# A planner with two DMA queues: beacon attention and a gated feed-forward part on one core

## The chip, the core and the metric

The kernel runs on one core of a Trainium2 chip, as one launch. The metric is the device time of that launch in microseconds. Five engines have an instruction queue each: TensorE (PE in the profile), VectorE (DVE), ScalarE (ACT), GpSimd (POOL) and SyncE (SP); transfers are started from SP's queue (the hardware queue q1 of the profile) and from POOL's (the software queue q0).

## The reference

```python
B, H, S, Nb, D = (8, 8, 576, 16, 64)
k_all = np.concatenate([beacon_k, k], axis=2)
v_all = np.concatenate([beacon_v, v], axis=2)
scores = scale * np.matmul(q, k_all.transpose(0, 1, 3, 2))
causal[:, Nb:] = np.triu(np.ones((S, S), dtype=bool), k=1)
scores = np.where(causal, -1000000000.0, scores)
a = np.exp(scores - scores.max(-1, keepdims=True))
a /= a.sum(-1, keepdims=True) + 1e-09
attn_out = np.matmul(a, v_all)
x = attn_out.transpose(0, 2, 1, 3).reshape(B * S, H * D)      # 4608 x 512
gate = np.maximum(x @ w_gate, 0.0)                             # 512 x 1536
return (gate * (x @ w_val)) @ w_out                            # 1536 x 512
```

All inputs and the output are float32.

## The kernel before

Attention is worked batch by batch (eight batches), two pairs of heads at a time (`quad`, g = 0 and 1). Queries, keys and values are loaded through eight staging tiles `st`, rounded to bf16 on GpSimd (in batch 0 also on VectorE), keys and queries are turned on TensorE (`turned`, line 538) and copied out of PSUM into `kT` and `qT`. Scores (line 809) are masked and their row minimum of the negated scores is taken on VectorE (757), exponentials come from ScalarE (764), reciprocals from VectorE (770), and the normalisation by GpSimd (775). The probabilities are transposed, on TensorE in batch 0 (885) and else by a DMA transpose on SP's queue (895), and multiplied by the values (905, 928). The results go to `xT`, from which the feed-forward part reads spans of 240 to 512 tokens: gate (966) and value products (971), their product on VectorE (982), the output product (997), an eviction and a store (1011).

The order of all this on every engine is not written by hand. Each piece is a `Task` with its engines, a modelled cost, what it depends on, the buffers that it holds and a priority; `Plan.order` simulates the program and emits each task when its turn comes. So what the planner believes about durations decides what stands ahead of what in each engine's queue, and each queue is worked in order on the chip. Where the plan has TensorE idle in the first part, it puts in filler matmuls on a spare bank (`fill`, line 1049). Value products of later batches may lie up to `LAZY` = 20 us behind feed-forward matmuls.

Transfers in the planner before: one number `wire` says when all that was issued will have moved. A load adds its `move` to it and lands `LAND` = 1.8 us later; weights, issued by GpSimd, add theirs to the same number. A new transfer waits until the wire is at most `BACKLOG` = 6 us ahead. Weights become due at `W0 + W_STEP * i`.

`HELD` names three loads of batch 1 that wait for the issue of a given weight, and `BEHIND` one load of batch 2 that waits for normalised probabilities of batch 1: the staging tile is first written by a one-element memset on GpSimd (548), and the load depends on that.

The batch's loads go in the order of a string: `K` and `Q` are the rest of the keys and queries, a digit a pair of heads (keys first, then queries), `v` one block of 128 value rows (the fifth has 80):

```python
for what in ORDER0 if b == 0 else "KQ0011v2233vvvv":
```

Of the kernel before, what the change touches and what calls it, by code (L numbers as in the profile page):

```python
# [12 lines left out]
ALU = mybir.AluOpType  # L13
# [22 lines left out]
TURN = (7,)  # L36
QUADS = 5
TLAZY = 8.0
TURN_FIRST = 100
TURN_LOAD = 1.5  # L40
# [15 lines left out]
W_ROWS = 4  # L56
W0 = 14.0
W_STEP = 1.4
W_ISSUE = 0.85
W_MOVE = 0.72  # L60
V_MOVE = 1.25
LAND = 1.8
N_ST = 8
# [10 lines left out]
VCAST = 9  # L74
STORES = 0

# [81 lines left out]
class Task:  # L158
    def __init__(self, engines, cost, run, deps, holds, prio, lag, part=0, lazy=0.0, move=0.0):
# [21 lines left out]


class Plan:

# [5 lines left out]

    def add(self, engines, cost, run, deps=(), holds=(), prio=0.0, lag=None, part=0, lazy=0.0, after=0.0, move=0.0):
        t = Task(engines if isinstance(engines, tuple) else (engines,), cost, run, deps, holds, prio, lag, part, lazy, move)
        t.ready = after
        for d in t.deps:
            d.users.append(t)
        self.tasks.append(t)
        return t

    def order(self):
        free = {}  # L200
        queue = {}
        for t in self.tasks:
            for e in t.engines:
# [6 lines left out]
        wire = 0.0  # L210
        part = 0
        free["DMA"] = 0.8
        done = []

        def begin(t, e):
            at = t.ready
            if e == "DMA" or t.move:
                at = max(at, wire - self.backlog)
            for h in t.holds:
                if h.tile is None:  # L220
                    if h.prev is not None:
                        continue
                    if h.next is not None:
                        first = h.slots.first_pairs(sum(x.next is not None for x in t.holds))
# [8 lines left out]
            return max(at, free[e]), at  # L233

        while True:
            best = None
            for e in queue:
                for t in queue[e]:
                    times = begin(t, e)
                    if times is None:  # L240
                        continue
                    at, could = times
                    late = 0
                    if e == "PE":
                        late = -1 if part and t.part == part else NEXT if part and t.part else 1 if part != t.part and at < t.ready + t.lazy else 0
                    key = (at, late, t.prio)
                    if best is None or key < best[0]:
                        best = (key, t, e)
            if best is None:
                break  # L250
# [19 lines left out]
            if e == "DMA":  # L270
                issue, move = cost
                if issue > 1.2:
                    wire = max(wire, at + 0.3) + move
                    free[e] = max(at + issue, wire - 0.2)
                else:
                    free[e] = at + issue
                    wire = max(wire, at + issue) + move
                end = max(wire, free[e]) + LAND
            else:
                if isinstance(cost, dict):  # L280
                    cost = cost[e]
                if e == "PE":
                    cost += SWITCH * (t.part != part)
                    part = t.part
                free[e] = end = at + cost
                if t.move:
                    wire = max(wire, end) + t.move
                    end = wire + LAND
            for h in t.holds:
                h.users -= 1  # L290
                if h.users == 0:
                    h.slots.give(end + (0.1 if e == "DMA" else LAGS[e] if t.lag is None else t.lag), h.tile)
            done.append(t)
            for u, then in [(u, end) for u in t.users] + [(u, free[e]) for u in t.soon]:
                u.ready = max(u.ready, then + (LAGS[e] if t.lag is None else t.lag))
                u.left -= 1
                if u.left == 0:
                    for x in u.engines:
                        queue[x].append(u)
        assert all(t.start is not None for t in self.tasks)  # L300
# [5 lines left out]
def kernel(  # L306
# [102 lines left out]
    def c_pool(n):  # L409
        return 0.245 + 0.00083 * n  # L410

    def c_pe(n):
        return 0.003 + n / 2400.0
# [74 lines left out]
    def weight(kind, ko, kos, n0, w, prio, work):  # L488
        d, s = {"g": (wg_r, wg_s), "v": (wv_r, wv_s), "o": (wo_r, wo_s)}[kind]
        x = add("POOL", W_ISSUE, lambda t: nc.gpsimd.dma_start(  # L490
            d[:, ko:ko + kos, n0:n0 + w], s[:, ko:ko + kos, n0:n0 + w]), (), (), work, 0.1, move=W_MOVE * kos * w / 512,
            after=W0 + W_STEP * len(weight_in) / KM)
# [13 lines left out]
    def new_batch(b, prio, work):  # L506
# [54 lines left out]
        def load_pair(kind, p, prio):  # L561
# [20 lines left out]
            if b in TURN:  # L582
                t.rows[kind, p] = [add("DMA", (1.22, 0.177 * 4), lambda _: nc.sync.dma_start_transpose(
                    dst.tile[:, p, c0:c0 + MAIN].rearrange("p (j n) -> p j n", j=4), h16.tile), (ca, zeros), (h16, dst), prio[0] - TURN_FIRST)]
                return
# [41 lines left out]
        def load_half(kind, g, half, prio):  # L627
# [24 lines left out]
        def load_rest(kind, prio):  # L652
# [36 lines left out]
        def load_v(c, prio):  # L689
            rows = min(P, SK - P * c)  # L690
            if b >= VCAST:
# [7 lines left out]

                t.rows["v", c] = add("POOL", W_ISSUE * (2 if c == 0 else 1), take, (batches[-1].rows["v", NC - 1],), (t.v,), prio[1], 0.1, move=V_MOVE * rows / P)  # L700
                return
# [31 lines left out]
    def softmax(t, parts, ph, prio, k):  # L733
# [38 lines left out]
        for i, (n, a) in enumerate(whole):  # L772
            def norm(x, i=i, n=n, a=a):
                one = ph.tile.rearrange("p a n -> p (a n)")[:, a:a + n]
                nc.gpsimd.tensor_scalar(one, one, at(8 + i), 1.0, ALU.mult, ALU.mult)  # L775

            outs.append(add("POOL", c_pool(n), norm, (r,), (ph,), prio + 0.001 * i + 0.0005 * k))
        return outs
# [89 lines left out]
    def finish(t, p, vals, ph, pt_s, blocks, on_pe, outs, prio):  # L868
# [89 lines left out]
    def ffn(m0, mt, deps, prio):  # L958
# [26 lines left out]
        for t0 in range(0, mt, P):  # L985
# [19 lines left out]
            for c in range(halves):  # L1005
# [3 lines left out]
                def store(_, c=c, osb=osb[c], rows=rows, t0=t0, w=w):  # L1009
                    q_ = nc.scalar if c or STORES else nc.sync  # L1010
# [72 lines left out]
```

## Time and profile before

| | |
|---|---|
| runs | 398.83, 404.41, 398.99 us; median 398.99 |
| profiled execution | span 403.9 us from first to last instruction; its own time is not listed beside the runs |
| busy | PE 390.9, DVE 282.5, ACT 266.7, POOL 233.8 us |
| mean TensorE clock granted | 0.989 |
| filler matmuls (line 1049) | 89 |
| SP queue q1 / POOL queue q0 | 63.46 MB / 4.72 MB |

The table of stretches gives for each stretch the length, then busy time and count of instructions for PE, PE's weight loads, DVE, ACT and POOL, then the granted clock of TensorE (1.00 is full speed), the mean busy share of the 16 DMA engines and GB/s. With a filter for one line and PE it gives PE alone. In the chain that ended last, each row is a start, a length and what the program's end hung on at that time. In a timeline, the bracket gives the idle time of the engine before the instruction and what ended it. Rows of transfers give count, size of one in KB and the median time from issue to landing.

### The profile page before, as it was taken

What the parts mean: (1) busy time and instruction counts of PE and PEld (TensorE: products, weight loads), DVE (VectorE), ACT (ScalarE), POOL (GpSimd) and SP (SyncE); (2) the same over time, 40 slices, a digit from 0 to 9 for tenths busy, and PEclk for the clock granted to TensorE, in tenths of its full rate; (3) what the DMA queues carried; (4) which work ended last, traced back from release to release, by engine and by line L of the source; (5) the groups of instructions that cost most, each with busy time, mean ns of one, the idle gap of its engine ahead of it and who ended that gap; (6) DMA issues with size and microseconds to landing.
All of it is one profiled execution on the core that took longest, in us unless ns stands there. A gap on an engine that the chain in (4) does not pass through costs nothing.

```text
span 403.9 us, 10330 instructions
## 1 busy us (share of the span) xinstructions
PE 390.9 (97%) x3471; PEld 203.8 (50%) x3471; DVE 282.5 (70%) x1011; ACT 266.7 (66%) x833; POOL 233.8 (58%) x453
## 2 busy tenths in 40 slices
PE   7969999999999989999999999999999999999996
PEld 4636865565454545554454444545444445444543
DVE  3859788897997778878777778678857843442432
ACT  2949879978866776959786787878765841330320
POOL 6877959969793885668687585855670730000000
PEclk9969999999999999999999999999999999999999
DMA  7999894999999899979998999799959655001102
GB/s 181 227 201 244 146 226 145 219 179 233 204 255 202 215 175 259 163 170 276 230 183 225 262 187 159 162 214 158 197 145 193 122 100 152 16 2 52 52 2 91
DMA packets 184101, 68.90 MB, mean 171 GB/s; under 512 B 158384, under 2 KB 179504, under 8 KB 184048
## 3 DMA queue, kind: packets, MB, share of 16 engines
q1 hardware_dynamic: 179216, 63.46, 74.5%
q0 software_dynamic: 4752, 4.72, 7.4%
q8 instruction: 27, 0.44, 0.5%
q14 instruction: 26, 0.21, 0.2%
q10 hardware_dynamic: 80, 0.07, 0.1%
HBM read 38.54 MB, written 9.44 MB: 119 GB/s over the span
## 4 chain that ended last, share of the span: by engine, by line
PE 87%; DMA 5%; ACT 4%; DVE 2%; issue 1%; POOL 0%; ACTq 0%; DVEq 0%
PE f L997 23%; PE f L971 22%; PE f L966 22%; PE f L809 7%; PE f L905 6%; ACT pb L764 3%; PE f L538 3%; DMA st<-in_v_dram 2%; DMA pTa<-pa 2%; PE f L1049 1%; PE f L885 1%; PE f L928 1%; DVE f L757 1%; DMA st<-in_k_dram 1%; PE f L859 1%
## 5 line engine op out<-in xcount | busy, mean ns | idle before, releaser
L775 POOL TENSOR_SCALAR pb<-pb,small 128x320 bf16<-128x320 bf16 (+8 forms) x272 | 141.8, 539 | 69.9 <-DVE small L770 67.3
L764 ACT ACTIVATE pb<-f,small 128x320 bf16<-128x320 f32 (+8 forms) x272 | 144.4, 552 | 22.5 <-DVE small L757 15.1
L757 DVE CUSTOM_DVE_ANT_0 f<-f,mask 128x576 f32<-128x576 f32 (+8 forms) x288 | 134.3, 512 | 13.8 <-PE f L809 6.5
L971 PE MATMUL f<-xT,wv_r 128*128 128x512 bf16 (+3 forms) x480 | 107.4, 358 | 0.0
L966 PE MATMUL f<-xT,wg_r 128*128 128x512 bf16 (+3 forms) x480 | 106.2, 358 | 0.0
L997 PE MATMUL f<-wo_r,hT 128*128 128x512 bf16 (+2 forms) x456 | 102.3, 374 | 0.0
L982 DVE TENSOR_TENSOR hT<-g,f 128x512 bf16<-128x512 f32 (+3 forms) x120 | 75.2, 631 | 36.9 <-PE f L971 33.8
L977 ACT ACTIVATE g<-f 128x512 f32<-128x512 f32 (+3 forms) x120 | 67.7, 567 | 48.3 <-PE f L966 44.3
L966 PEld LDWEIGHTS <-wg_r 128*128 128x128 bf16 x480 | 45.6, 98 | 44.9 <-issue 1.0
L997 PEld LDWEIGHTS <-hT 128*128 128x128 bf16 (+2 forms) x456 | 41.9, 100 | 46.7 <-issue 2.4
L971 PEld LDWEIGHTS <-wv_r 128*128 128x128 bf16 x480 | 43.3, 98 | 42.7 <-issue 3.4
L764 ACT ACTIVATION_READ_ACCUMULATOR pb<-f,small 128x1 f32 x272 | 60.4, 222 | 0.0
L527 POOL TENSOR_SCALAR h<-st 128x512 bf16<-128x512 f32 (+1 forms) x93 | 49.0, 542 | 10.5 <-DMA st<-in_k_dram 3.2
L757 DVE DVE_READ_ACCUMULATOR2_ANT small<- 128x1 f32 x296 | 41.2, 139 | 0.1
L809 PE MATMUL f<-kT,qT 64*64 64x64 bf16 (+7 forms) x640 | 35.9, 296 | 3.4 <-DVE xT L478 3.4
L478 DVE COPY osb<-f 128x512 f32<-128x512 f32 (+1 forms) x29 | 19.7, 681 | 26.9 <-PE f L997 26.8
L476 ACT CAST xT<-f 128x240 bf16<-128x240 f32 (+2 forms) x43 | 15.7, 375 | 25.3 <-PE f L905 24.9
L770 DVE RECIPROCAL small<-small 128x2 f32<-128x2 f32 (+3 forms) x136 | 20.4, 160 | 14.1 <-ACT pb L764 10.4
L809 PEld LDWEIGHTS <-qT 64*64 64x64 bf16 x640 | 14.5, 107 | 27.0 <-issue 22.3
L905 PE MATMUL f<-pTb,v 128*64 128x320 bf16 (+3 forms) x488 | 27.3, 254 | 0.3
L480 POOL TENSOR_SCALAR v<-st 128x512 bf16<-128x512 f32 (+1 forms) x38 | 23.1, 616 | 6.4 <-DMA st<-in_v_dram 6.4
L905 PEld LDWEIGHTS <-v 128*64 128x64 bf16 (+1 forms) x512 | 21.3, 110 | 9.1 <-issue 5.4
(62 smaller groups left out, 231.0 us busy)
## 6 DMA issues: line engine op xcount, KB each, us to landing
out_dram<-osb SPq DMA_DIRECT2D x34, 256.0 KB, 2.5
st<-in_k_dram SPq DMA_DIRECT2D x28, 256.0 KB, 4.6
st<-in_q_dram SPq DMA_DIRECT2D x28, 256.0 KB, 4.4
st<-in_v_dram SPq DMA_DIRECT2D x24, 256.0 KB, 5.3
st<-in_k_dram SPq DMA_DIRECT2D x16, 128.0 KB, 4.1
st<-in_q_dram SPq DMA_DIRECT2D x16, 128.0 KB, 3.2
st<-in_v_dram SPq DMA_DIRECT2D x8, 224.0 KB, 5.3
wg_r<-in_moe_w_gate_dram POOLq DMA_DIRECT2D x3, 512.0 KB, 7.1
```

The costliest lines, as they stand in the source:

```text
L480: nc.gpsimd.tensor_scalar(dst, src, 1.0, 1.0, ALU.mult, ALU.mult)
L527: (nc.gpsimd if x.engine == "POOL" else nc.vector).tensor_scalar(to, src, by, 1.0, ALU.mult, ALU.mult)
L757: nc.vector.tensor_tensor_reduce(out=view(i, n - m), in0=view(i, n - m), in1=msk, scale=1.0, scalar=at(7) if m < n else 3.0e38, op0=ALU.ad ...
L764: nc.scalar.activation(ph.tile.rearrange("p a n -> p (a n)")[:, a:a + n], view(i), AF.Exp, bias=at(i), scale=-1.0, accum_out=at(4 + i))
L775: nc.gpsimd.tensor_scalar(one, one, at(8 + i), 1.0, ALU.mult, ALU.mult)
L809: nc.tensor.matmul(banks[k][b_].tile[64 * i:64 * i + 64, off:off + n], t.q.tile[r, 2 * g + i, 64 * j:64 * j + 64], t.kT.tile[r, 2 * g + i, ...
L905: nc.tensor.matmul(ps.tile[64 * hh:64 * hh + 64, d0:d0 + w], t.v.tile[:rows, c, D * h:D * h + D], rhs(64 * hh), start=(c == 0), stop=(c == ...
L966: nc.tensor.matmul(psg.tile[:, :mt], wg_r[:, ki, nf * P:(nf + 1) * P], xT[:, ki, m0:m0 + mt], start=(ki == 0), stop=(ki == KM - 1))
L971: nc.tensor.matmul(psv.tile[:, :mt], wv_r[:, ki, nf * P:(nf + 1) * P], xT[:, ki, m0:m0 + mt], start=(ki == 0), stop=(ki == KM - 1))
L977: r = add("ACT", c_act(mt), lambda _, psg=psg, g=g: nc.scalar.activation(g.tile[:, :mt], psg.tile[:, :mt], AF.Relu), (a,), (psg, g), -1000 ...
L982: hid.append(add("DVE", c_dve(mt), lambda _, psv=psv, g=g, nf=nf: nc.vector.tensor_mul(hT[nf].tile[:, :mt], g.tile[:, :mt], psv.tile[:, :m ...
L997: nc.tensor.matmul(ps[c].tile[64 * c:64 * c + rows, :w], hT[nf].tile[:, t0:t0 + rows], wo_r[:, nf, w * c:w * c + w], start=(nf == 0), stop ...
```

## The change

The planner gets a class `Wire` with two queues, HW (SP) and SW (GpSimd). Every transfer becomes one or more jobs, each with a number of packets per DMA engine and a kind of packet. A queue works its jobs in order; alone at `ALONE` us per packet, and while both queues have work at the packets per us of `TOGETHER`, first for HW, then for SW. A transfer lands `LAND` after its last packet, and its users are woken by that event. At most eight jobs of the hardware queue are under way. The three holds in `HELD` go; `BEHIND` stays. Weights are due at 13, 16, ... 37 us. All engines start at 0.8 us of the plan. A task that may run on several engines is not given to one where another would finish it sooner. The normalisation takes its engine from `NORM`, which names GpSimd alone, as before. The option `STORES` goes; it was 0.

```diff
-HELD = {(1, 0): ("v", 0, 0), (1, 2): ("g", 0, 1024), (1, 4): ("v", 0, 1024)}
+HELD = {}
-W0 = 14.0
-W_STEP = 1.4
+W0 = 13.0
+W_STEP = 3.0
-W_MOVE = 0.72
-V_MOVE = 1.25
-LAND = 1.8
+LAND = 1.0
+HEAD = {"HW": 0.9, "SW": 1.2}
+ALONE = {256: 0.0182, 512: 0.03, 1024: 0.045, 2048: 0.075, "T": 0.01875, "W": 0.096}
+TOGETHER = {256: (12.0, 9.0), 512: (10.0, 8.7), 1024: (8.0, 8.2), 2048: (5.5, 7.0), "T": (12.0, 9.0)}
+NORM = [("POOL",)]
...
+class Wire:
+    def __init__(self):
+        self.now = 0.0
+        self.jobs = {"HW": [], "SW": []}
+    def load(self):
+        return sum(j.size * ALONE[j.runs] for j in self.jobs["HW"])
+    def run(self, until):
+        while True:
+            heads = {q: x[0] for q, x in self.jobs.items() if x and x[0].start <= self.now + 1e-9}
...
+            if len(heads) == 2:
+                both = TOGETHER[heads["HW"].runs]
+                rate = {"HW": both[0], "SW": both[1]}
+            else:
+                rate = {q: 1.0 / ALONE[j.runs] for q, j in heads.items()}
...
+    def sooner(self, t, x, e, at, begin):
+        other = begin(t, x)
+        return other is not None and (other[0] + t.cost[x], x) < (at + t.cost[e], e)
...
-                free.setdefault(e, 0.0)
+                free.setdefault(e, 0.8)
...
-            if e == "DMA" or t.move:
-                at = max(at, wire - self.backlog)
+            if e == "DMA":
+                if len(flying) >= 8 and flying[-8].task is not None:
+                    return None
+                at = max(at, wire.now + wire.load() - self.backlog)
...
+            ended = wire.run(best[0][0] if best is not None else 1e9)
+            if ended:
+                for j in ended:
...
+                    if t.jobs == 0:
+                        release(t, max(wire.now, j.end) + LAND, None, t.engine)
...
+                for n, (size, runs) in enumerate(jobs):
+                    q = "HW" if e == "DMA" else "SW"
+                    go = at + issue * (n + 1) / len(jobs) + HEAD[q]
+                    if runs == "T":
+                        go = max(at + HEAD[q], go - size * ALONE["T"])
+                    j = wire.put(q, size, runs, go, 0.0)
...
-            ld = add("DMA", (1.0, TURN_LOAD) if b in TURN else (0.5, 0.87), fetch, (held,), (st,), prio[0])
+            ld = add("DMA", (1.0, [(32, 256)] * 2) if b in TURN else (0.48, [(16, 1024)]), fetch, (held,), (st,), prio[0])
-            ld = add("DMA", (0.5, 0.95), fetch, (held,), (st,), prio[0])
+            ld = add("DMA", (0.53, [(32, 512)]), fetch, (held,), (st,), prio[0])
-            ld = add("DMA", (1.3, 0.96), fetch, (held,), (st,), prio[0])
+            ld = add("DMA", (1.35, [(32, 256), (8, 256)]), fetch, (held,), (st,), prio[0])
-            ld = add("DMA", (1.1 if c == 0 else 0.55, V_MOVE * rows / P), fetch, (held,), (st,), prio[0])
+            ld = add("DMA", (1.05, [(8, 256), (56, 256)]) if c == 0 else (0.5, [(rows / 2, 256)]), fetch, (held,), (st,), prio[0])
...
-            tr = [add("DMA", (max(1.22, 0.15 * blocks), 0.177 * blocks), lambda _: nc.sync.dma_start_transpose(
+            tr = [add("DMA", (max(1.22, 0.152 * blocks), [(8 * blocks, "T")]), lambda _: nc.sync.dma_start_transpose(
...
-                add(*(("ACT", 0.12) if STORES else ("DMA", (0.4, 0.78 / halves))), store, (ev,), (osb[c],), prio + OUT, move=0.78 / halves if STORES else 0.0)
+                add("DMA", (0.47, [(8 / halves, 2048)]), store, (ev,), (osb[c],), prio + OUT)
```

More of the change, by code (lines that the diff above doesn't have):

```diff
@@ L158, with __init__ @@
 class Task:
-    def __init__(self, engines, cost, run, deps, holds, prio, lag, part=0, lazy=0.0, move=0.0):
+    def __init__(self, engines, cost, run, deps, holds, prio, lag, part=0, lazy=0.0, move=()):
         self.part, self.lazy, self.move = part, lazy, move
@@ L180, in run, with __init__, put @@
         self.fill(self.n, self.tile)
+class Job:
+    def __init__(self, size, runs, start, end):
+        self.size, self.runs, self.start, self.end = size, runs, start, end
+class Wire:
+    def __init__(self):
+        self.now = 0.0
+        self.jobs = {"HW": [], "SW": []}
+    def put(self, queue, size, runs, start, end):
+        self.jobs[queue].append(Job(size, runs, start, end))
+        return self.jobs[queue][-1]
+    def load(self):
[3 more added lines that the diff above has]
+            heads = {q: x[0] for q, x in self.jobs.items() if x and x[0].start <= self.now + 1e-9}
+            later = [x[0].start for x in self.jobs.values() if x and x[0].start > self.now + 1e-9]
+            if not heads:
+                if not later or min(later) > until:
+                    self.now = max(self.now, until)
+                    return None
+                self.now = min(later)
+                continue
+            if len(heads) == 2:
[3 more added lines that the diff above has]
+                rate = {q: 1.0 / ALONE[j.runs] for q, j in heads.items()}
+            step = min(j.size / rate[q] for q, j in heads.items())
+            stop = min([until] + later)
+            if self.now + step > stop:
+                for q, j in heads.items():
+                    j.size -= rate[q] * (stop - self.now)
+                self.now = stop
+                if stop >= until:
+                    return None
+                continue
+            self.now += step
+            ended = []
+            for q, j in heads.items():
+                j.size -= rate[q] * step
+                if j.size <= 1e-9:
+                    self.jobs[q].pop(0)
+                    ended.append(j)
+            return ended
 class Plan:
@@ L189, in __init__, with add @@
         self.filled = 0.0
-    def add(self, engines, cost, run, deps=(), holds=(), prio=0.0, lag=None, part=0, lazy=0.0, after=0.0, move=0.0):
+    def add(self, engines, cost, run, deps=(), holds=(), prio=0.0, lag=None, part=0, lazy=0.0, after=0.0, move=()):
         t = Task(engines if isinstance(engines, tuple) else (engines,), cost, run, deps, holds, prio, lag, part, lazy, move)
@@ L209, in order @@
                     queue[e].append(t)
-        wire = 0.0
+        wire = Wire()
+        flying = []
         part = 0
-        free["DMA"] = 0.8
         done = []
@@ L233, in begin, with release, wake @@
             return max(at, free[e]), at
+        def release(t, end, then, e):
+            for h in t.holds:
+                h.users -= 1
+                if h.users == 0:
+                    h.slots.give(end + (0.1 if e == "DMA" else LAGS[e] if t.lag is None else t.lag), h.tile)
+            for u in t.users:
+                wake(u, end + (LAGS[e] if t.lag is None else t.lag))
+        def wake(u, at):
+            u.ready = max(u.ready, at)
+            u.left -= 1
+            if u.left == 0:
+                for x in u.engines:
+                    queue[x].append(u)
         while True:
@@ L243, in order @@
                     late = 0
+                    if len(t.engines) > 1 and any(self.sooner(t, x, e, at, begin) for x in t.engines if x != e):
+                        continue
                     if e == "PE":
@@ L270, in order @@
             if e == "DMA":
[L271 to L278, printed above, removed]
+                issue, jobs = cost
             else:
@@ L284, in order @@
                     part = t.part
[L285 to L292, printed above, removed]
-            done.append(t)
[L294 to L299, printed above, removed]
+                issue, jobs = cost, t.move
+            free[e] = end = at + issue
+            if jobs:
+                t.jobs = len(jobs)
+                for n, (size, runs) in enumerate(jobs):
[4 more added lines that the diff above has]
+                    j = wire.put(q, size, runs, go, 0.0)
+                    j.task = t
+                    if q == "HW":
+                        flying.append(j)
+                for u in t.soon:
+                    wake(u, end + LAGS[e])
+            else:
+                release(t, end, None, e)
+                for u in t.soon:
+                    wake(u, end + LAGS[e])
+            done.append(t)
         assert all(t.start is not None for t in self.tasks)
@@ L490, in weight @@
         x = add("POOL", W_ISSUE, lambda t: nc.gpsimd.dma_start(
[L491 removed]
+            d[:, ko:ko + kos, n0:n0 + w], s[:, ko:ko + kos, n0:n0 + w]), (), (), work, 0.1, move=[(8 * kos, "W")],
             after=W0 + W_STEP * len(weight_in) / KM)
@@ L582, in load_pair @@
             if b in TURN:
-                t.rows[kind, p] = [add("DMA", (1.22, 0.177 * 4), lambda _: nc.sync.dma_start_transpose(
+                t.rows[kind, p] = [add("DMA", (1.22, [(32, "T")]), lambda _: nc.sync.dma_start_transpose(
                     dst.tile[:, p, c0:c0 + MAIN].rearrange("p (j n) -> p j n", j=4), h16.tile), (ca, zeros), (h16, dst), prio[0] - TURN_FIRST)]
@@ L774, in norm @@
                 one = ph.tile.rearrange("p a n -> p (a n)")[:, a:a + n]
-                nc.gpsimd.tensor_scalar(one, one, at(8 + i), 1.0, ALU.mult, ALU.mult)
-            outs.append(add("POOL", c_pool(n), norm, (r,), (ph,), prio + 0.001 * i + 0.0005 * k))
+                (nc.vector if x.engine == "DVE" else nc.gpsimd).tensor_scalar(one, one, at(8 + i), 1.0, ALU.mult, ALU.mult)
+            outs.append(add(NORM[min(t.b, len(NORM) - 1)], {"POOL": c_pool(n), "DVE": c_norm(n)}, norm, (r,), (ph,), prio + 0.001 * i + 0.0005 * k))
         return outs
```

13 lines of the change are left out of this document (9 added, 4 removed).

## The prediction

> **What bounds the kernel now.** I read the page first, then a table of 10 us stretches for all engines and for the filler matmuls of line 1049 alone, then the chain that ended last, the timelines of PE and DVE around the one long gap, and the transfers.
>
> ```profile
> PE 390.9 (97%) x3471; PEld 203.8 (50%) x3471; DVE 282.5 (70%) x1011; ACT 266.7 (66%) x833; POOL 233.8 (58%) x453
> ...
> 0.00:10.00 10.00, 7.01 (x56) 4.36 (x56) 3.93 (x40) 2.45 (x3) 6.64 (x21) 1.00 0.75 181
> 10.00:20.00 10.00, 9.23 (x103) 6.20 (x101) 8.77 (x48) 9.71 (x42) 8.16 (x17) 1.00 1.20 226
> 20.00:30.00 10.00, 6.58 (x47) 3.45 (x44) 5.11 (x21) 4.44 (x13) 8.15 (x18) 0.66 1.22 202
> 30.00:40.00 10.00, 9.88 (x115) 6.73 (x112) 9.05 (x38) 9.83 (x31) 7.15 (x14) 1.00 1.19 249
> 40.00:50.00 10.00, 10.00 (x149) 8.37 (x146) 7.61 (x24) 8.98 (x25) 9.07 (x16) 1.00 0.79 143
> ```
>
> TensorE (the first busy column) is full from 40 us on. Before that, part of its busy time is filler:
>
> ```profile
> 0.00:10.00 10.00, 5.17 (x20) 1.00 0.75 181
> 10.00:20.00 10.00, 5.77 (x42) 1.00 1.20 226
> 20.00:30.00 10.00, 3.71 (x16) 0.66 1.22 202
> 30.00:40.00 10.00, 2.33 (x12) 1.00 1.19 249
> ```
>
> Useful work in the first 40 us is 32.7 - 17.0 = 15.7 us, so 24 us of TensorE time are lost there. Behind it lie 403.9 - 40 = 364 us of which nearly all is needed. An order of the program can therefore gain only in the head, and lose anywhere. The largest single loss in the head:
>
> ```profile
> 13.47 10.00 DMA st<-in_v_dram
> ...
> 23.48 0.42 DVE v L478
> 23.91 0.48 DVE xT L478
> ...
> 24.43 0.64 PE f L809 x3
> ...
> 26.53 1.18 PE f L1049 x5
> 27.71 0.62 PE f L809 x3
> 28.32 1.18 PE f L1049 x5
> 29.51 0.64 PE f L885 x6
> ...
> 23.48 0.42 DVE L478 CAST v<-st 80x512 bf16<-80x512 f32 x1 [4.20 <-DMA st<-in_v_dram]
> 23.83 0.54 DVE L478 COPY xT<-f 128x768 bf16<-128x768 bf16 x1
> ...
> 24.43 0.64 PE L809 MATMUL f<-kT,qT 64*64 64x512 bf16 x3 [3.42 <-DVE xT L478]
> ```
>
> The last value load of batch 0 landed 10.00 us after its issue. Its cast stood on DVE ahead of the eviction that frees a bank, so DVE waited 4.20 us and TensorE 3.42 us. Right behind it the granted clock (the column after POOL) is halved:
>
> ```profile
> 22.00:24.00 2.00, 0.00 (x0) 0.00 (x0) 0.52 (x2) 0.00 (x0) 1.58 (x3) 0.79 1.21 203
> 24.00:26.00 2.00, 1.57 (x12) 0.55 (x11) 2.00 (x10) 0.43 (x2) 1.46 (x3) 0.50 1.24 203
> 28.00:30.00 2.00, 2.00 (x16) 1.44 (x13) 0.84 (x3) 0.84 (x4) 1.61 (x4) 0.50 1.22 195
> ```
>
> **The time that the sum starts from.** The span is 403.9 us, and an execution is not shorter than its span. Of the three runs (398.83, 398.99, 404.41) only the last can hold it, so I take the profiled execution's own time as 404.4, 0.5 beyond the span (an estimate from those two numbers). The two others, and the median 398.99, are 5.4 us shorter.
>
> **The change, part by part.** What it removes: the one wire on which the planner moved all transfers one after the other. A value load that shares the engines with weights of 80 rows was planned to land 0.55 + 1.25 x 80/128 + 1.8 = 3.1 us after its start if the wire was free; it took 10.00. The new planner has two queues which slow each other: by its tables 12 packets of 256 B per us on each engine beside weights, and 1/0.0182 = 55 alone. The load's 40 packets then take 3.3 us instead of 0.7, and loads ahead of it lengthen by the same ratio. It should see the late landing and put the cast behind the bank's eviction.
>
> 1. *The gap*: -3.42 us of TensorE. Bounds: 0 if another late load takes its place, -4.20 if all of the DVE wait goes. I take -3.4, since the gap of TensorE is what the chain contains.
> 2. *The half clock*: from 24.43 to 30.15 the chain lies on PE alone, 5.7 us at half speed; without it 2.8 us less. Bounds 0 and -2.8 (0 if the time is given back as filler); taken -2.8.
> 3. *Loads of batch 1 no longer held*: three of four marker memsets (L548, 0.09 us each) go, and the loads behind them can start earlier:
>
> ```profile
> L548 POOL MEMSET st<- x4: 88/89/90, 16.9 to 75.8; 1x1 f32 x4
> SPq L572 <- POOL st L548: 9.6, 2, 6.2
> ...
> 40.00:42.00 2.00, 2.00 (x31) 1.46 (x29) 1.67 (x8) 1.89 (x5) 2.00 (x4) 1.00 0.20 32
> ...
> 52.82 0.63 PE L809 MATMUL f<-kT,qT 64*64 64x64 bf16 x16
> ```
>
> The sync queue waited 9.6 us for markers, and the transfers had a hole at 40 to 42 us (share 0.20). But TensorE is full there and its first scores of batch 1 come at 52.82, so most of it is hidden. What it can buy is the 2.33 us of filler at 30 to 40 us. Bounds 0 and -2.3; taken -1.2, the middle.
>
> 4. *Weights at 13, 16, ... 37 us*, instead of what the old wire let through:
>
> ```profile
> 14.33 1.10 POOL L490 DMA_DIRECT2D wg_r<-in_moe_w_gate_dram  x1
> 31.87 0.79 POOL L490 DMA_DIRECT2D wv_r<-in_moe_w_val_dram  x1
> 51.04 0.79 POOL L490 DMA_DIRECT2D wo_r<-in_moe_w_out_dram  x1
> ...
> 32.24 0.58 PE L966 MATMUL f<-xT,wg_r 128*128 128x240 bf16 x4
> ```
>
> Up to the first matmul of the feed-forward part at 32.24 GpSimd issued six weights (the first and the sixth are shown, and the ninth); by the new due times it is seven, at 0.79 us each, ahead of normalises that the values wait for. Bounds 0 (GpSimd idles in between) and +1.6 (two more in front of the last normalise); taken +0.8.
>
> 5. *Landings planned sooner.* A transpose of 25 blocks was planned at 0.3 + 0.177 x 25 + 1.8 = 6.5 us, now at 0.95 + 200 x 0.01875 + 1.0 = 5.7; a load of one pair at 0.5 + 0.87 + 1.8 = 3.2, now 0.48 + 0.9 + 0.72 + 1.0 = 3.1. Measured:
>
> ```profile
> st<-in_k_dram SPq DMA_DIRECT2D x28, 256.0 KB, 4.6
> st<-in_q_dram SPq DMA_DIRECT2D x28, 256.0 KB, 4.4
> pTb<-pb SPq DMA_TRANSPOSE x28, 6.6
> ...
> PE f L928 <- DMA pTa<-pa: 1.3, 1, 1.3
> ```
>
> So the long transposes may come 0.9 us after their new plan. Now TensorE waits once for a transpose, 1.3 us in all, because the value products may lag up to 20 us (LAZY) behind feed-forward matmuls. I take +0.3. Bounds: -1.3 (that wait goes) and +25 (28 x 0.9, no cover).
>
> 6. *The sooner rule for ACT or DVE, engines that start at 0.8 us, the unused branch of normalise, the store option*: 0, since every normalise ran on GpSimd already and TensorE is full behind 40 us; bounds -1 and +1, a couple of 0.5 us evictions like the row at 23.83.
>
> Sum for the profiled execution: -3.4 - 2.8 - 1.2 + 0.8 + 0.3 = -6.3, so 404.4 - 6.3 = 398.1. For an ordinary run: terms 1 and 2 are 6.2 us, while ordinary runs are shorter by 5.4. If these 5.4 are all parts of the two terms, 0.8 are left to gain; if ordinary runs keep the whole gap and lack the half clock and its consequences, 3.4 are. I take the middle, -2.1: 398.99 - 2.1 - 1.2 + 0.8 + 0.3 = 396.8 us.
>
> [...]
>
> **The rivals.**
>
> *The head closes up* (faster by over 2%). If DVE and ACT, busy 8.77 and 9.71 of 10 us at 10 to 20, kept that rate through 20 to 30 (5.11 and 4.44), ACT would save about 5.3 us; together with the filler of 30 to 40 (2.3) and the wait of 1.3 that is -8.9: 390.1. For it: the loss in the head is 24 us. Against: the weights then come no earlier, and an ordinary run has probably lost less than the profiled one.
>
> *Landings planned too soon* (slower). The place is the batch boundaries in the middle and the in-order queues of POOL and PE: a cast or a value product put where the plan sees data, with the data 0.9 us (transposes) to 1.4 us (pairs, 4.5 less 3.1) later. Each engine then waits with all that stands behind it: on POOL the normalises, and behind them SP, whose transposes stand ahead of the next loads. Half of 28 transposes exposed are 14 x 0.9 = 12.6 us: 396.8 + 12.6 = 409. For it: measured medians lie above the new plan. Against: medians hold queueing that the new wire models itself, and the lag of 20 us covers the products. It decides once attention falls so far behind that no feed-forward matmul is ready, as already for 1.3 us.
>
> *Weights crowd out batch 1* (slower).
>
> ```profile
> q0 software_dynamic: 1055, 1.05, 69.3%
> q1 hardware_dynamic: 3523, 0.91, 50.7%
> ...
> st<-in_v_dram SPq DMA_DIRECT2D x1, 160.0 KB, 10.0
> st<-in_q_dram SPq DMA_DIRECT2D x1, 128.0 KB, 10.9
> ```
>
> These are the transfers of 14 to 24 us, with four weights in flight: loads land after 10 to 11 us. With nine weights in 27 us instead of 37 this state lasts through the loads of batch 1. TensorE has the two first spans as cover, so scores at 52.82 may slip by several us unseen; a slip of 20 us with half covered costs 10: 407. It decides when gate and value products of batch 0 have run out before those scores.
>
> *Nothing moves*: the late cast stays ahead on DVE, or another takes its place, and the changes of order cancel: 399.
>
> **How the numbers follow.** The likeliest case, 396.8 with its own range 394 to 400, has 0.43; nothing moves 0.08; the head closes up 0.17; landings too soon 0.20; weights crowd out 0.12. Two per cent, about what a measurement of this kernel can tell from no change, are 391.0 and 407.0. So faster 0.17, same 0.51, slower 0.32. The range goes from 389.5 (the head closes up) to 409.5 (landings too soon, half exposed).
>
> **What would show it.** Right: no DVE wait of 4 us for a value load in the first 30 us, no half clock, first gate matmul at 27 to 30 us instead of 32.24, weights issued by 40 us, TensorE idle below 2 us in all behind 40 us, fillers below 17 us. Wrong: TensorE waits behind 40 us for transposes or casts that sum to several us; first scores of batch 1 later than 60 us; a gap of 3 us and half clock at another place of the head; POOL waiting for loads by far more than the old order did.

## The result, and the profile after

The changed kernel takes 420.5 us (median of four; 416.99 the lowest) beside 400.91 for the kernel before on the same chip: the ratio is 1.0471, 95% interval 1.0367 to 1.0575. It is slower by some 19 us where 2 us less had been forecast. (The ratio leaves out one run of the changed kernel, which took 2181.18 us for a reason that stays unknown, the other three being 416.99, 419.87 and 421.13; the kernel before has runs near 399 and runs near 404, so its median moves between 399 and 403 from one comparison to the next, and each ratio below is against the runs of it that were taken along with that kernel.) The profiled execution took 421.13 us with a span of 419.3.

The page of the changed kernel, and three of its stretches (columns as before: length, then busy time of PE, PE's weight loads, DVE, ACT, POOL; clock; DMA share; GB/s). The last row is the kernel before, from 120 to 140 us:

```profile
PE 392.1 (93%) x3417; PEld 203.9 (49%) x3460; DVE 273.2 (65%) x1000; ACT 275.9 (66%) x852; POOL 229.4 (55%) x442
...
70.00:80.00 10.00, 7.92 (x88) 4.91 (x87) 7.91 (x25) 6.11 (x21) 7.50 (x14) 0.88 1.07 243
...
120.00:140.00 20.00, 14.60 (x168) 8.11 (x172) 13.18 (x49) 11.23 (x40) 11.17 (x22) 0.89 0.97 209
...
220.00:240.00 20.00, 17.96 (x190) 8.52 (x191) 10.95 (x43) 12.27 (x41) 10.83 (x21) 0.91 0.86 147
...
120.00:140.00 20.00, 20.00 (x187) 9.94 (x185) 15.37 (x51) 14.52 (x48) 12.12 (x24) 1.00 0.97 214
```

TensorE's busy time is nearly what it was (390.9); the span has grown because it now stands idle in the middle, 5.4 us of 20 from 120 to 140, where the kernel before was full. And the clock falls behind such gaps (0.88 to 0.91 in these stretches, against 1.00). Most transfers take about as long from issue to landing as before: keys 4.8 us (4.6 before), long transposes 6.4 (6.6), though queries take 5.1 (4.4).

```profile
st<-in_k_dram SPq DMA_DIRECT2D x28, 256.0 KB, 4.8
pTb<-pb SPq DMA_TRANSPOSE x28, 6.4
wg_r<-in_moe_w_gate_dram POOLq DMA_DIRECT2D x3, 512.0 KB, 10.0
wo_r<-in_moe_w_out_dram POOLq DMA_DIRECT2D x3, 512.0 KB, 13.0
```

The weights land later after their issue than they did (before, gate weights after 7.1 us and output weights after 7.2). The head, on the other hand, became what the forecast said. First the first gate product, then the fillers of 20 to 30 and 30 to 40 us:

```profile
25.40 0.58 PE L1052 MATMUL f<-xT,wg_r 128*128 128x240 bf16 x4
...
20.00:30.00 10.00, 3.31 (x21) 1.00 1.21 236
30.00:40.00 10.00, 0.76 (x4) 1.00 1.21 212
```

The first gate product starts 6.8 us earlier than before (32.24), at full clock, and there is no wait of 4 us on VectorE. The first scores of batch 1 come at 49.20 us (52.82 before). What follows loses this gain several times over. TensorE's longest gaps in the changed kernel, from its timeline (in brackets the idle time and who ended it), and the totals from the table of waits:

```profile
75.86 0.88 PE L991 MATMUL f<-pTb,v 128*64 128x128 bf16 x16 [1.73 <-DMA pTb<-pb]
...
133.03 0.67 PE L1014 MATMUL f<-pTa,v 128*128 128x32 bf16 x20 [1.39 <-DMA pTa<-pa]
137.44 0.61 PE L624 MATMUL f<-ident,h 128*128 128x128 bf16 x4 [2.88 <-POOL h L613]
...
216.32 0.36 PE L991 MATMUL f<-pTb,v 128*64 128x128 bf16 x6 [1.27 <-DMA pTb<-pb]
226.19 0.67 PE L1014 MATMUL f<-pTa,v 128*128 128x32 bf16 x20 [1.83 <-ACT pb L850]
...
PE f L991 <- DMA pTb<-pb: 5.2, 6, 1.7
PE f L624 <- POOL h L613: 4.1, 3, 2.9
PE f L1014 <- DMA pTa<-pa: 3.1, 3, 1.4
```

They are waits for transposes and for loaded rows that GpSimd had to round first: all of it data that came by SP's queue. The rounding ahead of the gap at 137.44 had itself waited 5.59 us for its load. The row at 226.19 names ScalarE, but this product reads `pTa`, whose transpose landed at 226.14. Behind 40 us the gaps add up to 18.3 us, against 1.7 in the kernel before.

**Against the plan.** Each kernel carries its own forecast: the start that `Plan.order` gave each task. I matched the planned starts with the trace, in order: gate products on TensorE (by their weight loads) and transfers on SP's queue (by their issues). The table gives the start on the chip less the planned start, in us, as a mean over the 10 us of plan time from the time named. A positive number is lateness. The last three kernels are experiments told below.

```
plan time                     60    90   110   130   150   200   240   300
before           PE gate     5.8   6.1   6.0   6.0   7.7   7.9   8.4   8.1
                 SP issue    5.6   4.8   3.6   5.0   6.2   6.9   7.5   8.4
changed          PE gate     1.9   5.6   6.5  14.1  15.1  17.7  21.5  24.3
                 SP issue    2.3   6.5  10.7  14.7  14.4  20.8  22.9  24.5
changed, old     PE gate     3.5   3.4   3.5   3.5   3.6   3.7   3.8   3.7
 durations (e5)  SP issue    3.2   3.7   3.2   3.0   2.8   4.3   3.9   4.1
before, new      PE gate     2.3   5.4   5.4   9.6   9.4   9.8  11.1  12.0
 durations (e7)  SP issue    3.0   5.9   7.2  10.3  10.6  11.1  10.7  12.3
best (e10)       PE gate     0.3   0.4   0.0   0.1   0.0   0.5   0.4   0.2
                 SP issue    0.5   1.6   0.4   1.6   0.1   1.4   2.1  -0.2
```

The two plans end at almost the same time, 393.8 and 393.2 us. The old one comes true but for the gap in the head (5.8 us at once) and some 2 us later. The new one starts well and then loses 22 us. Before, SP was mostly less late than TensorE: its long transposes were planned longer (4.4 us) than they took (4.07 us in the median, 4.22 in the mean). In the changed kernel SP is later: 10.7 against 6.5 us at 110. The jump of TensorE to 14.1 follows.

The plans of the experiments do not all end at the same time: those of e5, e10 and e11 end between 393.9 and 394.2 us, but those of e3 and e7 end at 398.2 and 398.6, and that of e12 at 400.9. There, some of the loss stands in the plan itself and not in its lateness.

### The profile page after: what moved, and what is told of

The parts are those of the page before. It is cut to its first block, busy times and chain, and to the rows that moved or that the text cites. A ratio compares the mean times of both kernels' runs of the same rounds, so it can differ in the third digit from the quotient of the medians.

```text
span 419.3 us, 10266 instructions
## 1 busy us (share of the span) xinstructions
PE 392.1 (93%) x3417; PEld 203.9 (49%) x3460; DVE 273.2 (65%) x1000; ACT 275.9 (66%) x852; POOL 229.4 (55%) x442
## 4 chain that ended last, share of the span: by engine, by line
PE 68%; DMA 16%; POOL 5%; DVE 4%; issue 4%; SPq 2%; ACT 1%; POOLq 0%; DVEq 0%; ACTq 0%
PE f L1083 23%; PE f L1057 16%; PE f L1052 15%; DMA pTb<-pb 7%; PE f L895 5%; PE f L991 4%; DMA wv_r<-in_moe_w_val_dram 2%; PE f L624 2%; DMA pTa<-pa 2%; DVE f L843 2%; POOL pb L861 2%; POOL xT L861 2%; DMA st<-in_k_dram 1%; DMA st<-in_q_dram 1%; DVE hT L1068 1%
## 5 line engine op out<-in xcount | busy, mean ns | idle before, releaser
L850 ACT ACTIVATE pb<-f,small 128x320 bf16<-128x320 f32 (+8 forms) x272 | 143.4, 547 | 16.6 <-DVE small L843 14.4
L1083 PE MATMUL f<-wo_r,hT 128*128 128x512 bf16 (+3 forms) x441 | 101.8, 380 | 1.5 <-issue 1.0
L1063 ACT ACTIVATE g<-f 128x512 f32<-128x512 f32 (+3 forms) x120 | 66.5, 560 | 49.3 <-PE f L1052 40.0
L1083 PEld LDWEIGHTS <-hT 128*128 128x128 bf16 (+3 forms) x456 | 42.2, 101 | 48.6 <-issue 5.6
L850 ACT ACTIVATION_READ_ACCUMULATOR pb<-f,small 128x1 f32 x272 | 59.1, 217 | 0.0
L613 POOL TENSOR_SCALAR h<-st 128x512 bf16<-128x512 f32 (+1 forms) x86 | 45.7, 546 | 19.5 <-DMA st<-in_k_dram 5.6
L562 ACT COPY osb<-f 128x512 f32<-128x512 f32 (+3 forms) x24 | 13.6, 566 | 33.2 <-PE f L1083 32.9
L895 PE MATMUL f<-kT,qT 64*64 64x512 bf16 (+7 forms) x640 | 35.1, 299 | 0.2
L562 ACT CAST xT<-f 128x320 bf16<-128x320 f32 (+2 forms) x53 | 18.9, 360 | 19.2 <-PE f L991 17.1
L624 PE MATMUL f<-ident,h 128*128 128x128 bf16 (+1 forms) x224 | 21.9, 229 | 5.2 <-POOL h L613 4.1
```

The source lines that it names most:

```text
L562: nc.scalar.copy(dst, src)
L613: (nc.gpsimd if x.engine == "POOL" else nc.vector).tensor_scalar(to, src, by, 1.0, ALU.mult, ALU.mult)
L850: nc.scalar.activation(ph.tile.rearrange("p a n -> p (a n)")[:, a:a + n], view(i), AF.Exp, bias=at(i), scale=-1.0, accum_out=at(4 + i))
L895: nc.tensor.matmul(banks[k][b_].tile[64 * i:64 * i + 64, off:off + n], t.q.tile[r, 2 * g + i, 64 * j:64 * j + 64], t.kT.tile[r, 2 * g + i, ...
L1063: r = add("ACT", c_act(mt), lambda _, psg=psg, g=g: nc.scalar.activation(g.tile[:, :mt], psg.tile[:, :mt], AF.Relu), (a,), (psg, g), -1000 ...
L1083: nc.tensor.matmul(ps[c].tile[64 * c:64 * c + rows, :w], hT[nf].tile[:, t0:t0 + rows], wo_r[:, nf, w * c:w * c + w], start=(nf == 0), stop ...
```

## Experiments

"Idle" is the sum of TensorE's gaps behind 40 us in the profiled execution of each run; 1.7 before, 18.3 changed. The traces of the changed kernel, of e1 to e4 and of e9 to e11 each lack 43 to 45 of the 1416 feed-forward matmuls that the others hold. The holes, mostly of 0.05 and 0.16 us, count as idle: some 2 to 4 us in each of these sums. The diffs are shortened to the values that change.

**Only the landing put back (e1).**

```diff
-LAND = 1.0
+LAND = 1.8
```

> The changed kernel with one constant altered: a transfer lands 1.8 us behind its last packet in the plan, as before the change, instead of 1.0. Theory A (data planned at its best-case landing, so that in-order queues wait for it): the late landings of transposes and loads fall inside the plan's slack, TensorE's idle time behind 40 us goes from some 16 us to below 5, and the time is 400 to 407. Rival B (the loss comes from the loads and weights of the head, holds removed and 3 us steps): nothing of the middle changes, 415 to 422. Rival C (any new order is worse than the one the hand-set priorities were fitted to): TensorE keeps 10 us or more of idle time at other places, 410 to 420.

414.33 us, ratio 1.0302 (1.0171 to 1.0434), idle 16.8: in the range of rival C, far from A's. About a third of the loss goes, but not the cause. Two of its gaps alone take 6.6 us, the first at a place where the changed kernel has none:

```profile
52.83 0.61 PE L624 MATMUL f<-ident,h 128*128 128x128 bf16 x4 [3.35 <-POOL h L613]
...
138.21 0.72 PE L1014 MATMUL f<-pTa,v 128*128 128x32 bf16 x20 [3.29 <-DMA pTa<-pa]
```

Theory A in its simple form, a landing planned too early, fell here.

**Only the transposes planned longer (e2).**

```diff
-"T": 0.01875      max(1.22, 0.152 * blocks)
+"T": 0.0225       max(1.22, 0.18 * blocks)
```

> The changed kernel with only the long DMA transposes planned longer: 0.0225 us per packet and 0.18 us of issue per block, 4.5 us for 25 blocks instead of 3.8 (measured between their issues when back to back: 3.7 to 4.8). Theory A, if the transposes carry the loss: TensorE's waits for pTb and pTa (8.3 us in the changed kernel) fall below 3, time 403 to 411. If the loads carry it: the waits for casts on GpSimd stay, time 413 to 420. Rivals B and C: 413 to 422.

414.83 us, ratio 1.0334 (1.0203 to 1.0464), idle 14.4. The time lies in the range given for the loads, and for rivals B and C. But the waits went another way than was expected for the loads: TensorE's waits for casts on GpSimd halve (4.1 to 2.1 us), and value products still wait for transposes, though these are now planned about as long as they take:

```profile
PE f L991 <- DMA pTb<-pb: 7.0, 7, 3.1
```

This points to what stands ahead of them in SP's queue.

**Holds and weight times of before (e3).**

```diff
-HELD = {}   W0 = 13.0   W_STEP = 3.0
+HELD = {(1, 0): ("v", 0, 0), (1, 2): ("g", 0, 1024), (1, 4): ("v", 0, 1024)}   W0 = 14.0   W_STEP = 1.4
```

> The changed kernel with the three holds back and weights due at 14.0 in steps of 1.4 us as before. Theory A: the middle still waits, 412 to 422, and the head loses a little of its gain. Rival B: this is the cause, so 398 to 405. Rival C: 410 to 425, with waits at other places.

429.26 us, ratio 1.0664 (1.0524 to 1.0805): above every range. The head is not the cause; with the holds and the old weight times back it loses what it had gained (first gate product at 32.79 us). The loads of batch 1 then come so late that TensorE waits 3.40 us for them at 50 us:

```profile
50.53 0.69 PE L624 MATMUL f<-ident,h 80*128 80x80 bf16 x4 [3.40 <-POOL h L613]
```

Rival B fell.

**The kernel before with short landings and transposes (e4).**

```diff
-LAND = 1.8    0.177 * blocks
+LAND = 1.0    0.155 * blocks
```

> The kernel before with its own one-wire planner, but landings and transposes planned as short as the change plans them: 1.0 us behind the wire instead of 1.8, and 0.155 us per block instead of 0.177 (25 blocks land after 5.2 instead of 6.5 us). Theory A: TensorE begins to wait behind 40 us, 5 to 15 us in all, time 406 to 418. Rival B: the head is that of before, 398 to 405. Rival C: 405 to 420 without more waits for transfers than for other engines.

408.15 us, ratio 1.0138 (1.0009 to 1.0266), idle 9.0, as theory A expected. The time lies in C's range too, but the waits behind 40 us are mostly for transfers (3.5 us for transposes, 1.2 for rounded loads), which C did not expect. The old planner has the same fault as soon as its durations are cut, though this order of the head has no gap of 3 us.

These four left open whether new orders are always worse (rival C) or whether something common to landings, loads and transposes is planned too fast. Compared with the plan, loads and transposes were not so much too short one by one as late at their issue (the table above). That gave theory A2: the service of SP's queue is planned too fast. Issues in the trace support it; this is the row of the long transposes in the changed kernel (durations min, median, max in ns), where the plan takes 3.8 us for each. Below it is the row of the kernel before, whose plan took 4.4:

```profile
L981 SPq DMA_TRANSPOSE pTb<-pb x28: 3717/4080/6252, 63.8 to 337.2; - x28
...
L895 SPq DMA_TRANSPOSE pTb<-pb x28: 3742/4068/5971, 71.2 to 331.1; - x28
```

The new constant is close to the least; half of them take 4.08 us and more. Their mean is 4.23 us, so the 28 take 12 us more on SP's queue than planned. The chip served them alike in both kernels; only the plan changed.

**The old durations in the new planner (e5).**

```diff
-ALONE = {256: 0.0182, 512: 0.03, 1024: 0.045, 2048: 0.075, "T": 0.01875, "W": 0.096}
+ALONE = {256: 0.0215, 512: 0.03, 1024: 0.054, 2048: 0.0975, "T": 0.0221, "W": 0.096}
-max(1.22, 0.152 * blocks)
+max(1.22, 0.177 * blocks)
```

> The changed kernel with the hardware queue's durations per transfer put back to about those of the old planner, and the landing left at 1.0 us: 0.0215 us per packet of 256 B, 0.054 of 1 KB, 0.0975 of 2 KB, 0.0221 per packet of a transpose and 0.177 us of issue per block. Theory A2 (not the landing but the service rate of SP's queue is planned too fast: the queue falls behind the plan by a per cent of its own length, and the engines follow): SP's issues are no longer later against the plan than TensorE is, TensorE's idle time behind 40 us is below 6 us, time 400 to 408. Theory A (landing alone): 412 to 420. Rival C (any new order has stalls of its own): 410 to 418 with SP not late.

402.36 us, ratio 1.007 (1.0045 to 1.0096), idle 0.5, in the range of A2. This takes back 4.0 of the 4.7% with two queues, short landing and no holds left in place. One gap remains, in the head, ahead of 40 us, with the clock halved for 3.4 us behind it (0.996 in the mean of the span):

```profile
PE 388.7 (97%) x3460; PEld 202.7 (51%) x3460; DVE 266.1 (67%) x990; ACT 280.9 (70%) x862; POOL 229.0 (57%) x442
...
33.72 0.58 PE L1057 MATMUL f<-xT,wv_r 128*128 128x240 bf16 x4 [2.27 <-DMA wv_r<-in_moe_w_val_dram]
```

**The old landing as well (e6).** The diff of e5 and `LAND = 1.8`.

> As the run with the old durations, and the landing at 1.8 us as well, so both parts of the old slack in the new planner. A2 with A: the least idle time of all variants, 398 to 404, the head as in the changed kernel. A2 alone: the same as with the durations alone, 400 to 408. Rival C: 408 to 418.

401.24 us, ratio 1.002 (0.9939 to 1.01), idle 1.9, so not the least of all as was expected: no difference from the kernel before that can be told, nor a clear one from e5. With the durations right, the landing is worth at most about a microsecond.

**The new durations in the old planner (e7).**

```diff
-0.177 * blocks   pairs 0.87   V_MOVE = 1.25    rest 0.96   stores 0.78
+0.15 * blocks    pairs 0.72   V_MOVE = 1.165   rest 0.73   stores 0.6
```

> The kernel before, one wire, holds, weights and landing of 1.8 us as they were, only the durations shortened as the change does: transposes 0.15 us per block instead of 0.177 (3.75 for 25 blocks), pairs 0.72 instead of 0.87, values 1.165 instead of 1.25, the rest rows 0.73 instead of 0.96, stores 0.6 instead of 0.78. Theory A2: SP's issues fall behind TensorE's slip by 1 to 3 us in the middle and TensorE idles 5 to 12 us behind 40 us: 404 to 415. Theory A: the old landing covers it, 398 to 404. Rival C: 400 to 415 with SP ahead as in the kernel before.

415.65 us, ratio 1.0401 (1.0365 to 1.0437), idle 13.1, a little more than A2 expected, and at full clock (1.0 in the profiled execution). Holds, weights, landing and the single wire are those of before. Its waits and its transposes:

```profile
PE f L905 <- DMA pTb<-pb: 5.8, 4, 2.8
PE f L538 <- POOL h L527: 3.6, 5, 1.5
PE f L928 <- DMA pTa<-pa: 2.6, 3, 1.3
...
L895 SPq DMA_TRANSPOSE pTb<-pb x28: 3736/4311/6201, 67.4 to 335.1; - x28
```

The waits are those of the changed kernel, in nearly its sizes, and in the table SP is behind TensorE again. In the old planner, shorter durations alone make most of the loss; part of it is the later end of the plan (398.6 against 393.8 us), the rest lateness. In the new one, longer durations alone take it away. The old landing of 1.8 does not cover it.

**The small rules alone (e8).** The kernel before with engines that start at 0.8 us in the plan, and with the rule on two engines.

> The kernel before with the two other rules of the change and nothing of the new wire: engines start at 0.8 us in the plan, and a task is not given to an engine where another would finish it sooner. Theories A and A2: the middle stays as before, 396 to 404. Rival C: another order, 403 to 415.

406.44 us, ratio 1.0183 (1.016 to 1.0206), idle 1.8. For A and A2 a miss in the time, which lies in C's range, though the middle is clean as they expected. The head has a longer form of the old gap:

```profile
25.03 0.53 PE L911 MATMUL f<-xT,v 128*64 128x128 bf16 x6 [4.50 <-DVE xT L484]
```

So a new order by itself can cost 2%, which is rival C's part of the truth; this one did not cost 5%, and nothing in the middle.

**Loads and stores long, transposes short (e9).**

```diff
-ALONE = {256: 0.0182, 512: 0.03, 1024: 0.045, 2048: 0.075,
+ALONE = {256: 0.0215, 512: 0.03, 1024: 0.054, 2048: 0.0975,
```

> The changed kernel with the durations of loads and stores put back (0.0215 us per packet of 256 B, 0.054 of 1 KB, 0.0975 of 2 KB), transposes and landing as the change has them. With the run that altered the transposes alone, this divides the cause. If the loads carry it: TensorE's idle time behind 40 us below 5 us, 400 to 407. If it needs both (each takes away part of the lateness, and the queue falls behind as long as either is short): 406 to 416, waits for transposes in the middle.

414.2 us, ratio 1.0331 (1.0215 to 1.0447), idle 12.5: the case that needs both. With e2 this divides the cause: loads alone 414.2, transposes alone 414.8 (there planned 2% longer still than in e5), both 402.4. Each half takes away 1.4 of the 4.7%, and the two together 4.0. That fits one queue worked in order (in the changed kernel all 231 transfers of SP's queue landed in the order of their issue): as long as either kind is planned too short, the whole queue runs late.

**The weights' service (e10).** The diff of e5, and:

```diff
-TOGETHER = {256: (12.0, 9.0), 512: (10.0, 8.7), 1024: (8.0, 8.2), 2048: (5.5, 7.0), "T": (12.0, 9.0)}
+TOGETHER = {256: (12.0, 7.8), 512: (10.0, 7.6), 1024: (8.0, 7.2), 2048: (5.5, 6.2), "T": (12.0, 7.8)}
-W0 = 13.0   W_STEP = 3.0
+W0 = 12.0   W_STEP = 2.5
```

> The changed kernel with the old durations (as in the run with these alone), and two edits for its last long gap, TensorE's 2.27 us for a value weight at 33.7 us: the software queue beside loads at 7.8, 7.6, 7.2 and 6.2 packets per us instead of 9.0, 8.7, 8.2 and 7.0 (weights landed 3 us behind their plan), and weights due at 12.0 in steps of 2.5 us. Theory A2: the gap and the half clock behind it go, idle time behind 40 us stays below 3 us, 396 to 401, a little faster than the kernel before. Rival C: a new gap elsewhere, 401 to 408.

398.0 us, ratio 0.9935 (0.9887 to 0.9984): faster than the kernel before by some 0.6%, and than the changed one by 22 us. Between the lowest runs of the two the difference is smaller (397.39 against 398.56). Idle 3.6, in 44 pieces of 0.16 us and less; as many matmuls are missing from this trace, so it shows no wait of TensorE behind 40 us at all. TensorE keeps the plan within 0.5 us at all the times of the table, and the clock is never halved within the span. Of the waits shown, the first and the third lie ahead of 40 us:

```profile
PE 384.9 (97%) x3427; PEld 203.5 (51%) x3471; DVE 266.8 (67%) x995; ACT 279.2 (71%) x859; POOL 228.7 (58%) x440
...
core 0: 395.9 us, clock 1.000
...
PE f L1135 <- POOL mask L510: 1.9, 1, 1.9
PE f L1083 <- issue: 1.3, 8, 0.2
PE f L624 <- DVE h L613: 1.1, 2, 0.7
```

**Only the step between weights (e11).** The diff of e5 and `W_STEP = 2.5`.

> The changed kernel with the old durations and only the step between weights altered, 2.5 us instead of 3.0. If the weights' real service time sets the gap at 33.7 us, it stays or grows, since the software queue is worked in order and no faster: 400 to 405. If their issue sets it, it shrinks: 397 to 401.

401.46 us, ratio 1.0007 (0.9963 to 1.0052). The gap at 33.7 us is gone in its trace too, and the span is 397.5 us, but the median stays in the range that stood for a gap that remains. What the other runs of it lost is open.

**The holds once more (e12).** e10 with `HELD` as before the change.

> The best version so far (old durations, slower weights beside loads, weights from 12.0 in steps of 2.5 us) with the three holds back. If removing the holds was worth the 1.2 us that the forecast gave it: 398.5 to 400.5. If, in this planner, they cost more, since the loads of batch 1 wait while the software queue is full anyway: 401 to 408, with more filler before 60 us and no more waits for transfers behind it. If they protect something that the free loads collide with: below 397.

405.82 us, ratio 1.0153 (1.011 to 1.0195), 8 us behind e10. Filler matmuls from 80 to 100 us, first in e10, then here, and the first scores of batch 1, in e10 and here:

```profile
80.00:100.00 20.00, 1.05 (x5) 1.00 1.05 246
80.00:100.00 20.00, 4.66 (x32) 1.00 1.09 226
...
48.34 0.63 PE L895 MATMUL f<-kT,qT 64*64 64x64 bf16 x16
58.09 0.63 PE L895 MATMUL f<-kT,qT 64*64 64x64 bf16 x16
```

Holding the loads makes batch 1 ten microseconds late, and TensorE is short of work some 30 us later. The filler was expected before 60 us and came at 80 to 100. The plan knew most of this: it ends at 400.9 us against 394.2 in e10.

**All runs together.** The kernels that plan SP's transfers with the old durations (before, e5, e6, e8, e10, e11, e12) idle 0.5 to 3.7 us behind 40 us. Those with any of them shortened (changed, e1, e2, e3, e4, e7, e9) idle 9.0 to 23.7. Orders differ within both groups, so a new order alone does not make the waits in the middle.

## Why the prediction was wrong

*The head (terms 1 and 2): right in kind.* The late value cast no longer stands in VectorE's way, the first half clock is gone, and gate products start at 25.40 us. I expected 27 to 30. TensorE's slip against its plan at 60 us fell from 5.8 to 1.9.

*The holds (term 3): right in sign, too small.* 1.2 us was taken, bounded by filler before 40 us. In the repaired planner they are worth some 8 (e12 against e10), since TensorE is short of work at 80 to 100 us, a place that the forecast did not look at.

*The weights (term 4): +0.8 taken, near in size by luck.* The term counted GpSimd's issue time ahead of normalises. What came is another wait: TensorE stands 0.9 us at 34.36 for value weights, which landed 1.5 to 4.0 us behind the plan although they were issued within 2 us of it. So the software queue beside loads was slower than its table.

*Landings planned sooner (term 5): the step that failed.* I took +0.3 with a bound of +25, because value products may lag by 20 us. The lag did not protect. By the kernel's code it only lets feed-forward matmuls go first while the plan is made; on the chip the order is fixed, and TensorE waits where the plan believed that data would be there. (No run changed `LAZY`, so this reason is read from the code.) Idle behind 40 us rose by 16.6 us. Half clock went from 6.8 to 13.7 us, another 3.4 us of matmul time. The head gave back 4.3 us (2.1 of idle, 2.2 of filler). That makes 15.7, and the span grew by 15.4. I had also put the shortening in the landing of one transfer (0.9 us each). The runs show it in the service of the queue: 0.3 us (median) to 2.5 us (longest) too little for each long transpose, 12 us in all, and something for the loads, which no view gives but e9 shows to be worth as much. Both add up along a queue that is worked in order, until TensorE waits.

*The small rules (term 6): 0 within 1 taken; +1.8% measured by themselves* in the old planner (e8), through another order of the head.

*The rival "landings planned too soon"* named the place, the kind of wait and the sign, and stood at 409 with a chance of 0.20. It assumed half of the transposes exposed, with no clock to lose and no loads in the sum, so it too fell short of the time. Of the signs given for a wrong forecast, the first one, waits behind 40 us for transposes and casts, is what the profile shows. The rival "weights crowd out batch 1" did not come: the first scores of batch 1 are 3.6 us earlier than before. (Its due times span 24 us, 13 to 37, and not 27.)

*The time that the sum starts from* was a little off. In all runs on record the time is 1.7 to 2.2 us beyond the span, not 0.5, so the profiled execution of the kernel before took about 405.6 us (an estimate from these) and is none of the three runs. This moves the forecast by less than 1 us.

## What to carry to other kernels

Where a program orders in-order queues by a model, the model's errors are not symmetric: here, the new planner with the old, longer durations stood within 1% of the kernel before (e5, e6), and transfers planned too short stopped an engine and all that stood behind it (4 to 5%). In these kernels a duration near the least that the trace shows (3.8 us planned for a long transpose, 3.72 the least) was too short for a busy queue (4.23 in the mean), so plan the sustained rate, for every kind of transfer on the queue. And compare plan and trace queue by queue: the queue whose lateness runs ahead of the others' is the first to suspect of being modelled too fast.

## What the runs showed of the hardware

Some gaps of TensorE of about two microseconds were followed by half clock. In the changed kernel it was at half from 77.51 us for 3.4 us, behind the 1.73 us gap that ended at 75.86 (mean 0.88 in its stretch above); from 135.53 for 6.8 us, behind the 1.39 us gap that ended at 133.03 and begun within the 2.88 us gap that ended at 137.44; and from 227.69 for 3.4 us, behind the 1.83 us gap that ended at 226.19. In e5 it was at half for 3.4 us behind the 2.27 us gap that ended at 33.72. Not every such gap was followed by it. In e3 those of 2.16, 2.46 and 2.48 us (ended at 115.03, 172.81 and 292.02) were not: behind them matmuls of 128x512 ran at full pace, four in 1.03 us at 117.86 and at 173.47, eight in 1.89 at 293.70. So in these traces the length of the gap alone does not decide; what does was not shown.

The weights on the software queue took longer to land where they were issued closer together: in the changed kernel, with nine weights issued within 26 us, the first landed 7.7 us after its issue and the last 13.8. In the kernel before, with nine in 37 us, all landed after 6.6 to 9.1 us.
